# 35 steps of the attention, in place of 18, take their squares from DRAM, transposed at the load; transfer figures of the scheduler changed

## The chip, the cores and the metric

The program runs on one core of a Trainium2 chip. The metric is the device time of one launch in microseconds (us). An execution under the profiler is read beside it. PE is TensorE (matmuls; PEld its weight loads), DVE is VectorE, ACT is ScalarE, POOL is GpSimd, and SP is SyncE, which issues almost every DMA.

## What is computed

```python
scores = scale * np.matmul(z, z.transpose(0, 2, 1))      # batch 4, seq 3072, d_qk 64
attn = np.maximum(scores, 0.0) ** 2                      # symmetric: z against itself
x = u * np.matmul(attn, v)                               # d_model 256
...                                                      # mixture of experts: 8 experts, capacity N // E * 2
...                                                      # keeps the first tokens of each expert, 256 -> 1024 -> 256
...                                                      # second network: 256 -> 2048 -> 256 on every token
```

The matrix `attn` of a batch is symmetric: the block for queries A and keys B is the transpose of the block for queries B and keys A.

## The kernel before, in words

The first part is the attention of the first 3,456 tokens. It runs in seven chunks of queries: chunks 0 to 5 are 512 queries each of the first batch, chunk 6 is 384 queries of the second. A chunk has 24 steps, one for 128 keys. An ordinary step is: two score matmuls of 512 columns (`scores`, L584); on ACT a relu out of PSUM into a tile `own` (L1015) and a square in place (L1021); a cast of the square to the matmul type on ACT or DVE (L113, L940) and, on DVE, the remainder of that cast (`rest`, L116), each into a tile of kind "rounded" (`ownr`, or the tiles `win` and `wout`, lent until chunk 6); and six matmuls that add to the output (`attend`, L124 to L127). Steps are three ahead in scores (`LEAD`).

18 steps have no score of their own. In chunks 3, 4 and 5, for keys that are the queries of chunks 0, 1 and 2, two steps in four are *mirrored*: the square was computed in the earlier chunk with the roles exchanged. There, in 36 source steps, DVE transposes 256 columns of the square in blocks of 32 by 32 (L1035), and four DMAs on SP (`m_store`, L617) write the tile to DRAM (`mir`) in pieces of 128 bytes so that it lies turned. The mirrored step then loads 128 rows of 2 KB with one DMA (`m_load`, L624).

Around this, DVE *narrows* the weights of the second network from 64 bits (`narrowing`, L1293 to L1335): eight loads of 1 MB into `raw` (L1279), each followed by two chains of nine DVE operations and by four stores to DRAM (L1351). Other work of DVE is the routing of each chunk's tokens (L656 to L859). After a chunk its rows are scattered by POOL into expert buffers. After chunk 6 come the first expert, which shares the time with the last routing, and then seven more experts and the second network; none of that is touched by the change.

The order of all this is set by a planner in the kernel (`Conductor`). It holds a list of jobs with a pace (estimated time on the engine), what they wait for, a step by which they are needed (`need`, `tail`), and a step before which they are not begun (`gate`). It plays time forward, gives each engine the job that can start first, and writes instructions in that order. The engines then run the order as it was written, each one in order: one instruction that waits holds up all behind it on its engine. The planner's figures for a DMA are `sync` (SP's time to issue), `moved` (time in the DMA engines) and a latency; they move no data by themselves, only the order.

Of the kernel before, what the change touches and what calls it, by code (L numbers as in the profile page):

```python
# [31 lines left out]
def tile_attn_moe_ffn(  # L32
# [256 lines left out]
    class Job:  # L289

        def __init__(
            self, on, pace, do, after=(), need=None, tail=0.0, gate=0, takes=None, ring=None,
            load=0.0, wait=None, kind="plain",
        ):
            self.on = on if isinstance(on, dict) else {on: pace}
            self.do, self.need, self.tail, self.gate = do, need, tail, gate
            self.takes, self.ring, self.load, self.wait = takes, ring, load, wait
            self.kind = kind
            self.after = [d if isinstance(d, tuple) else (d, 0.0) for d in after if d is not None]
            self.then, self.left, self.end, self.ran, self.buffer = [], 0, None, None, None  # L300
            self.placed = False

    class Conductor:

        SAME, CROSS, LATER = 0.03, 0.07, {"PE": 0.08, "ACT": 0.095, "DVE": 0.09}
        BANKS, WINDOW = 4, 16

# [29 lines left out]
        def spare(self, x):  # L337
            best = None
            for b in self.buffers:
                if b["kind"] != x.kind or b["until"] is not None and self.at >= b["until"]:  # L340
                    continue
                t = 0.0
                for u in b["users"]:
                    if u.end is None:
                        break
                    t = max(t, u.end)
                else:
                    if best is None or t < best[0]:
                        best = (t, b)
            return best  # L350

        def start(self, x, e):
            if x.left or self.at < x.gate:
                return None
            t = self.free[e]
            for d, more in x.after:
                t = max(t, d.end + more + (self.SAME if d.ran == e else self.CROSS))
            if x.wait is not None:
                w = x.wait()
                if w is None:  # L360
                    return None
                t = max(t, w + self.CROSS)
            if x.takes is not None:
                b = self.spare(x)
                if b is None:
                    return None
                t = max(t, b[0] + self.CROSS)
            if x.ring is not None and len(self.rings) >= self.BANKS:
                for u in self.rings[-self.BANKS]:
                    if u.end is None:  # L370
                        return None
                    t = max(t, u.end + self.CROSS)
            return t
# [15 lines left out]
        def choose(self, e):  # L389
# [11 lines left out]
            while live:  # L401
# [8 lines left out]
                else:  # L410
# [3 lines left out]
                    if len(x.on) > 1 and e == "DVE":  # L414
                        other = self.slack("ACT", max(self.free["ACT"], t))
                        if self.slack(e, t + pace, x) < max(0.0, other):
                            live = [c for c in live if c[2] is not x]
                            continue
# [16 lines left out]
        def place(self, e, t, x):  # L435
# [9 lines left out]
            if e == "SP":  # L445
                self.dma = max(self.dma, t + pace) + x.load
                x.end = self.dma + 2.0
            else:
                x.end = t + pace + self.LATER[e]
# [45 lines left out]
    def stage(att, flow):  # L495
# [95 lines left out]

        SOURCES, MIRRORED, MT, MC = (0, 1, 2), (3, 4, 5), QA // P, 2
        lm = flow == "first"
        if lm:
            mir = {
                c: dram.tile([len(MIRRORED), MC * P, QA], F32, name=f"mir{c}") for c in SOURCES
            }
# [12 lines left out]
        def mirrored(c, k):  # L610
            return lm and c in MIRRORED and k // MT in SOURCES and k % MT >= MT - MC

        def m_store(c, k, t):
            m, q = k // MT - MIRRORED[0], k % MT * P
            to = mir[c][m][:, q:q + P].rearrange("(b y) (l p) -> l y b p", y=SQ, p=SQ)
            for l in range(MT):
                nc.sync.dma_start(  # L617
                    out=to[l],
                    in_=t[l * SQ:(l + 1) * SQ].rearrange("y (b p) -> y b p", p=SQ),
                )  # L620

        def m_load(c, k, w):
            r = (k % MT - MT + MC) * P
            nc.sync.dma_start(out=w, in_=mir[k // MT][c - MIRRORED[0]][r:r + P, :])  # L624

# [8 lines left out]
        def route(c, b, q0, nq, accs, us, done, ready, where, freed, last):  # L634
# [215 lines left out]
            chain("g", lambda: nc.vector.reciprocal(out=t["g"], in_=t["g"]), k=20)  # L850
            puts, prior = [], prev
            for j in range(n):
                def scaled(j=j):
                    row, g = t["row"], t["g"]
                    nc.vector.tensor_scalar(
                        out=row[:, j, 0:TOK], in0=row[:, j, 0:TOK], scalar1=g[:, j, :],
                        scalar2=None, op0=ALU.mult,
                    )
                    nc.gpsimd.tensor_copy(  # L859
# [13 lines left out]

                prev = prior
                chain("row", scaled, pace=0.27, k=23)
            return listed

        def mm(n, count=1):
# [14 lines left out]
        def sync(packets):  # L893
            return 0.3 + packets * 0.0009

# [3 lines left out]
        def work(chunks, fresh, more=None, warm=None):  # L899
# [3 lines left out]

            LEAD = 3 if more else 2
            steps = [(c, k) for c in range(len(chunks)) for k in range(NK)]
# [28 lines left out]
            )  # L934

            def cast_by(x, out, src):
                if x.ran == "ACT":
                    rounded(out, src)
                else:
                    nc.vector.tensor_copy(out=out, in_=src)  # L940

# [39 lines left out]
            for i, (c, k) in enumerate(steps):  # L981
# [9 lines left out]
                )  # L991
                source = bool(mirrors) and c in SOURCES and k // MT in MIRRORED
                users = [cast, al]
                if (c, k) in mirrors:
                    w = Job(
                        "SP", sync(P), None, need=a_item, tail=9.0, gate=max(0, a_item - 18),
                        takes=users, load=moved(P, 2048),
                    )

                    def do(buf, s=s, c=c, k=k):  # L1000
                        s["a"] = buf
                        m_load(c, k, s["a"])

                    w.do = do
                else:
# [20 lines left out]
                    if source:  # L1026
                        t = add("DVE", dve_turn(MC * P), None, after=[w], need=a_item, tail=-3.0)
                        users.append(t)
                        put = add("SP", 4 * sync(MC * P), None, after=[t], need=a_item, tail=-3.5,
                                  load=moved(MC * P * 4, 128))  # L1030
                        t.takes = [put]

                        def do(buf, s=s):
                            s["t"] = buf[:, :MC * P]
                            nc.vector.transpose(out=s["t"], in_=s["a"][:, QA - MC * P:QA])  # L1035

                        t.do = do
                        put.do = lambda s=s, c=c, k=k: m_store(c, k, s.pop("t"))
                        stored[c, k] = put
# [17 lines left out]
                before(attended[c, k], cast, (al, -mm(nq, 4)))  # L1057
                if (c, k) in mirrors:
                    before(w, *(stored[k // MT, q] for q in range(c * MT, (c + 1) * MT)))

# [189 lines left out]
        def narrowing(ctx):  # L1250
            W, EVERY = 512, 16
            add, total, chains, loads = ctx["add"], ND * F2 // (2 * 512) + NF2 // 4, {}, []
# [21 lines left out]
            for n in range(total):  # L1274
# [6 lines left out]
                for q in range(2):  # L1281
# [3 lines left out]
                    def op(pace, fn, after=(), takes=None, kind="plain"):  # L1285
                        x = Job("DVE", pace, fn, after=[*ops[-1:], *after], takes=takes, kind=kind)
                        ops.append(x)
                        return x
# [44 lines left out]
                    def o8(buf, t=t):  # L1333
                        t["n0"] = buf
                        nc.vector.tensor_copy(out=buf, in_=t["af"])  # L1335

# [3 lines left out]

                    x1 = op(fast, o1, [load], [])
                    x2 = op(wide, o2)
                    x3 = op(fast, o3, takes=[])
                    x4, x5, x6, x7 = op(wide, o4), op(wide, o5), op(fast, o6), op(wide, o7)
                    x8 = op(fast, o8, takes=[], kind="rounded")
                    x9 = op(wide, o9, takes=[], kind="rounded")
# [22 lines left out]
        def fills(ctx):  # L1369
            add, where = ctx["add"], ctx["where"]  # L1370

# [21 lines left out]
            for i in range(FIRST // NZ):  # L1393
                add("SP", sync(NZ), partial(zero, i), after=[x],
                    gate=where["s", (1, 2 * i)], load=moved(NZ, 1024))

# [413 lines left out]
```

## Time and profile before

| | |
|---|---|
| time, median of 3 runs | 734.85 us (734.74 to 735.48) |
| the profiled execution | 735.21 us, span 733.4 us, mean granted clock 0.997 |
| PE, DVE, ACT busy | 717.3 (98%), 576.2 (79%), 584.5 (80%) us |
| the attention | 0 to about 317 us of the span |
| DMA packets | 151,807, of them 102,150 under 512 B |

The span is from the first to the last instruction of the profiled execution. PE is busy nearly all of it, so a change is felt where it alters what PE has to do or makes it wait. A matmul that the profile shows as 389 ns overlaps the next; how often one starts is the better measure.

### The profile page before, as it was taken

The page shows a single profiled execution, that of the slowest core. Times are in us where ns is not written, and L with a number is a line of the kernel's source. Part 1 is how long each engine was busy: PE and PEld are TensorE (multiplying, and loading weights), DVE is VectorE, ACT ScalarE, POOL GpSimd, SP SyncE. Part 2 cuts the span into 40 slices and gives each one's busy share as a digit, 9 for nine tenths or more (in the row PEclk, how much of TensorE's full clock was granted, in tenths as well). Part 3 has the DMA queues.
Part 4 walks back from the last instruction along what each step waited for, and adds up shares of the span by engine and source line. Part 5 has one row for each costly group of instructions (what it writes and reads, how often), then busy time and mean ns, then how long its engine had stood idle before and what let it go on. Part 6 is the DMA issues. An engine that isn't in the chain of part 4 may idle for free. (4 is left out here: it accounts for less than half of the span.)

```text
span 733.4 us, 11565 instructions
## 1 busy us (share of the span) xinstructions
PE 717.3 (98%) x3800; PEld 646.3 (88%) x3800; DVE 576.2 (79%) x1259; ACT 584.5 (80%) x1188; POOL 67.9 (9%) x108
## 2 busy tenths in 40 slices
PE   8999998999999999999999999999999999999996
PEld 5888886878888889998899999999999999999995
DVE  7988966998998988876967777777777777777782
ACT  7999997878868699957867777777778787788891
POOL 1000202002040120210000101001001001001011
PEclk9999999999999999999999999999999999999998
DMA  7739839487375455507660430710802504300000
GB/s 180 222 61 275 234 61 268 73 212 236 112 206 172 118 168 173 198 26 242 231 180 0 133 91 10 220 16 22 223 1 75 170 0 144 123 1 22 0 23 23
DMA packets 151807, 90.69 MB, mean 124 GB/s; under 512 B 102150, under 2 KB 140588, under 8 KB 151232
## 3 DMA queue, kind: packets, MB, share of 16 engines
q1 hardware_dynamic: 149296, 83.43, 41.2%
q0 software_dynamic: 2448, 6.49, 2.5%
q8 instruction: 31, 0.51, 0.3%
q14 instruction: 32, 0.26, 0.1%
HBM read 52.87 MB, written 35.94 MB: 121 GB/s over the span
## 5 line engine op out<-in xcount | busy, mean ns | idle before, releaser
L1632 PE MATMUL o<-wout,gh 128*128 128x512 f32 x384 | 139.3, 394 | 0.0
L1607 DVE SCALAR_TENSOR_TENSOR t<-x,t 128x384 f32<-128x384 f32 x128 | 71.4, 558 | 83.9 <-ACT t L1604 82.5
L1602 ACT ACTIVATE m<-h 128x384 f32<-128x384 f32 x128 | 62.6, 489 | 68.8 <-PE h L127 68.4
L1636 PE MATMUL o<-wout,gl 128*128 128x256 f32 x384 | 107.2, 280 | 0.2 <-DVE gl L116 0.2
L1015 ACT ACTIVATE own<-s 128x512 f32<-128x512 f32 (+1 forms) x150 | 85.2, 568 | 26.4 <-PE s L584 21.4
L1021 ACT ACTIVATE own<-own 128x512 f32<-128x512 f32 (+1 forms) x150 | 92.2, 615 | 4.2
L124 PE MATMUL h<-xh,win 128*128 128x384 f32 x256 | 86.2, 337 | 0.5 <-DVE g L1610 0.3
L125 PE MATMUL h<-xh,win 128*128 128x384 f32 x256 | 85.6, 334 | 0.0
L1632 PEld LDWEIGHTS o<-wout,gh 128*128 128x128 f32 x384 | 71.9, 188 | 11.1
L1610 DVE SCALAR_TENSOR_TENSOR g<-h,t 128x384 f32<-128x384 f32 x128 | 71.3, 557 | 4.4
L1636 PEld LDWEIGHTS o<-wout,gl 128*128 128x128 f32 x384 | 72.7, 189 | 1.1 <-DVE gl L116 0.9
L1603 ACT ACTIVATE x<-m 128x384 f32<-128x384 f32 x128 | 67.3, 526 | 4.1
L116 DVE TENSOR_TENSOR gl<-g,gh 128x384 fp32r<-128x384 f32 x128 | 70.0, 547 | 0.2 <-ACT gh L113 0.2
L127 PE MATMUL acc<-ownr,vs 128*128 128x512 f32 (+1 forms) x216 | 64.5, 379 | 3.5 <-DVE ownr L116 3.5
L113 ACT ACTIVATE gh<-g 128x384 fp32r<-128x384 f32 x128 | 65.2, 509 | 1.0 <-DVE g L1610 0.9
L127 PE MATMUL h<-xl,win 128*128 128x384 f32 x256 | 65.7, 337 | 0.0
L1604 ACT ACTIVATE t<-m 128x384 f32<-128x384 f32 x128 | 65.1, 508 | 0.0
L584 PE MATMUL s<-zs 128*128 128x512 f32 (+1 forms) x150 | 58.6, 391 | 0.0
L584 PE MATMUL s<-zw,zs 128*128 128x512 f32 (+1 forms) x150 | 57.2, 382 | 0.0
L124 PEld LDWEIGHTS h<-xh,win 128*128 128x128 f32 x256 | 48.0, 188 | 6.3 <-DVE g L1610 1.2
L124 PE MATMUL acc<-ownr,vs 128*128 128x512 f32 (+1 forms) x140 | 52.1, 372 | 0.0
L125 PE MATMUL acc<-ownr,vs 128*128 128x512 f32 (+1 forms) x140 | 51.9, 371 | 0.0
(153 smaller groups left out, 1655.2 us busy)
## 6 DMA issues: line engine op xcount, KB each, us to landing
raw<-in_moe_w_dram SPq DMA_DIRECT2D x16, 1024.0 KB, 6.3
out_dram<-fill SPq DMA_DIRECT2D x32, 384.0 KB, 6.9
vr<-in_v_dram SPq DMA_DIRECT2D x24, 256.0 KB, 4.4
mir<-own SPq DMA_DIRECT2D x144, 32.0 KB, 1.7
own<-mir SPq DMA_DIRECT2D x18, 256.0 KB, 2.8
raw<-in_moe_w_in_dram SPq DMA_DIRECT2D x4, 1024.0 KB, 6.1
raw<-in_moe_w_out_dram SPq DMA_DIRECT2D x4, 1024.0 KB
win<-win_d SPq DMA_DIRECT2D x8, 512.0 KB, 5.6
```

What stands on the lines that cost most here:

```text
L116: nc.vector.tensor_tensor(out=out, in0=src, in1=fp(hi), op=ALU.subtract)
L124: nc.tensor.matmul(out=ps, lhsT=hi, rhs=rh, start=first, stop=False)
L125: nc.tensor.matmul(out=ps, lhsT=lo, rhs=rh, start=False, stop=False)
L127: nc.tensor.matmul(out=ps, lhsT=hi, rhs=rl, start=False, stop=last)
L584: nc.tensor.matmul(out=ps, lhsT=zs[:, k * P:(k + 1) * P], rhs=w, start=(i == 0), stop=(i == 1))
L1015: nc.scalar.activation(out=s["a"][:, :nq], in_=s.pop("ps"), func=ACTF.Relu)
L1021: nc.scalar.activation(out=a, in_=a, func=ACTF.Square)
L1603: nc.scalar.activation(out=self.x, in_=self.m, func=ACTF.Exp, scale=-1.0)
L1607: nc.vector.scalar_tensor_tensor(out=self.t, in0=self.x, scalar=1.0, in1=self.t, op0=ALU.add, op1=ALU.mult)
L1610: nc.vector.scalar_tensor_tensor(out=self.g, in0=self.ps, scalar=0.0, in1=self.t, op0=ALU.max, op1=ALU.add)
L1632: both = lambda: nc.tensor.matmul(out=o, lhsT=hi[:, sl], rhs=w.rearrange("p a d -> p (a d)"), start=(f == 0), stop=(f == NF2 - 1),)
L1636: one = lambda: nc.tensor.matmul(out=o[:, 0:D], lhsT=lo[:, sl], rhs=w[:, 0, :], start=False, stop=False)
```

## The change

It replaces one way of passing a square through DRAM by another and uses it for more steps.

- Which steps: the table `MC` gives, for source chunk and target chunk, how many of each four steps are mirrored (2 or 3). Its 15 entries sum to 35 mirrored steps: 2, 6, 9, 8 and 10 in chunks 1 to 5. (The few words that came with the change say 34.)
- At the source: no DVE transpose. After the square one DMA stores its last 256 or 384 columns as rows of 1,024 or 1,536 bytes. 60 source steps store, 20 of them in chunk 0.
- At the target: four DMAs, each of 512 pieces of 128 bytes, load the tile with its blocks in turned places, and DVE transposes 512 columns in place, block by block (L1020 of the new file). Loads may begin 13 items ahead of the step (18 before).
- Figures: `sync` is 0.32 + 0.00034 us a packet (0.3 + 0.0009 before), landing is counted 2.5 us after the transfer (2.0), and SP jobs that no step needs wait until the planner's DMA queue is all but empty.
- Narrowing: its first operation is placed 4.0 us after the planned landing of its `raw` load; a load comes every 14 steps (16); its buffers are taken only where more than two are free (`modest`); its cast may go to ACT. The scaling of routed rows may go to ACT as well. The clause with `EASE` = 9.0 asks whether `slack` exceeds 9.0, which is the most that `slack` returns.
- The nine writes of zeros to the output (`out_dram<-fill`) that stood in chunk 1 and just behind it are allowed from chunk 6 on.

```diff
+                    spares += 1
                     if best is None or t < best[0]:
                         best = (t, b)
-            return best
+            return best if spares > x.modest else None
...
+            if e == "SP" and x.need is None:
+                t = max(t, self.dma - 0.5)
...
-                        if self.slack(e, t + pace, x) < max(0.0, other):
+                        if other > self.EASE or self.slack(e, t + pace, x) < max(0.0, other):
...
-                x.end = self.dma + 2.0
+                x.end = self.dma + 2.5
...
-        SOURCES, MIRRORED, MT, MC = (0, 1, 2), (3, 4, 5), QA // P, 2
+        MT = QA // P
+        MC = {(0, 1): 2, (0, 2): 3, (1, 2): 3, (0, 3): 3, (1, 3): 3, (2, 3): 3, (0, 4): 2, (1, 4): 2, (2, 4): 2, (3, 4): 2, (0, 5): 2, (1, 5): 2, (2, 5): 2, (3, 5): 2, (4, 5): 2}
...
         def mirrored(c, k):
-            return lm and c in MIRRORED and k // MT in SOURCES and k % MT >= MT - MC
-
-        def m_store(c, k, t):
-            m, q = k // MT - MIRRORED[0], k % MT * P
-            to = mir[c][m][:, q:q + P].rearrange("(b y) (l p) -> l y b p", y=SQ, p=SQ)
-            for l in range(MT):
+            return lm and k % MT >= MT - MC.get((k // MT, c), 0)
+
+        def m_store(c, k, a):
+            to = mir[c, k // MT]
+            r = k % MT * P
+            nc.sync.dma_start(out=to[r:r + P, :], in_=a[:, QA - MC[c, k // MT] * P:QA])
+
+        def m_load(c, k, w):
+            n = MC[k // MT, c]
+            x = (k % MT - MT + n) * P
+            for s in range(0, P, SQ):
                 nc.sync.dma_start(
-                    out=to[l],
-                    in_=t[l * SQ:(l + 1) * SQ].rearrange("y (b p) -> y b p", p=SQ),
-                )
-
-        def m_load(c, k, w):
-            r = (k % MT - MT + MC) * P
-            nc.sync.dma_start(out=w, in_=mir[k // MT][c - MIRRORED[0]][r:r + P, :])
+                    out=w[s:s + SQ].rearrange("p (t y) -> p t y", y=SQ),
+                    in_=mir[k // MT, c][:, x + s:x + s + SQ].rearrange("(t p) y -> p t y", p=SQ),
+                )
...
-            return 0.3 + packets * 0.0009
+            return 0.32 + packets * 0.00034
...
-            LEAD = 3 if more else 2
+            LEAD, AHEAD = (3 if more else 2), 13
...
-                source = bool(mirrors) and c in SOURCES and k // MT in MIRRORED
+                source = bool(mirrors) and MC.get((c, k // MT))
                 users = [cast, al]
                 if (c, k) in mirrors:
-                    w = Job(
-                        "SP", sync(P), None, need=a_item, tail=9.0, gate=max(0, a_item - 18),
-                        takes=users, load=moved(P, 2048),
+                    w = Job("DVE", dve_turn(nq), None, need=a_item, tail=1.5)
+                    users.append(w)
+                    load = add(
+                        "SP", 4 * sync(nq), None, need=a_item, tail=8.0, gate=max(0, a_item - AHEAD),
+                        takes=users, load=moved(4 * nq, 128),
+                        after=[stored[k // MT, q] for q in range(c * MT, (c + 1) * MT)],
                     )
                     def do(buf, s=s, c=c, k=k):
                         s["a"] = buf
-                        m_load(c, k, s["a"])
+                        m_load(c, k, buf)
+
+                    load.do = do
+                    before(w, load)
+
+                    def do(s=s):
+                        nc.vector.transpose(out=s["a"], in_=s["a"])
...
-                        t = add("DVE", dve_turn(MC * P), None, after=[w], need=a_item, tail=-3.0)
-                        users.append(t)
-                        put = add("SP", 4 * sync(MC * P), None, after=[t], need=a_item, tail=-3.5,
-                                  load=moved(MC * P * 4, 128))
-                        t.takes = [put]
-
-                        def do(buf, s=s):
-                            s["t"] = buf[:, :MC * P]
-                            nc.vector.transpose(out=s["t"], in_=s["a"][:, QA - MC * P:QA])
-
-                        t.do = do
-                        put.do = lambda s=s, c=c, k=k: m_store(c, k, s.pop("t"))
+                        put = add("SP", sync(P), None, after=[w], need=a_item, tail=-1.0,
+                                  load=moved(P, source * 512))
+                        users.append(put)
+                        put.do = lambda s=s, c=c, k=k: m_store(c, k, s["a"])
                         stored[c, k] = put
...
-            W, EVERY = 512, 16
+            W, EVERY = 512, 14
...
-                    x1 = op(fast, o1, [load], [])
+                    x1 = op(fast, o1, [(load, 4.0)], [])
...
+                    x8.on["ACT"] = act(W)
...
-                    gate=where["s", (1, 2 * i)], load=moved(NZ, 1024))
+                    gate=where["s", (last, 2 * i)], load=moved(NZ, 1024))
```

What the change does to the order is shown at three places. PE at the start of chunk 3, from the transposition of chunk 2's tokens (`xps`) on; `s` is a score, `acc` the output, `vs_144` holds the values of keys 2 and 3 of the chunk. Before:

```order
L670 MATMUL xps<-iw,ur 128x136 x8
L584 MATMUL s<-zs 128x512
L584 MATMUL s<-zw,zs 128x512
L124 MATMUL acc_1746<-ownr_180,vs_144 128x512
L125 MATMUL acc_1746<-ownr_180,vs_144 128x512
L124 MATMUL acc_1747<-ownr_180,vs_144 128x512
L125 MATMUL acc_1747<-ownr_180,vs_144 128x512
L127 MATMUL acc_1746<-ownr_176,vs_144 128x512
L127 MATMUL acc_1747<-ownr_176,vs_144 128x512
```

And now:

```order
L676 MATMUL xps<-iw,ur 128x136 x8
L124 MATMUL acc_1656<-ownr_187,vs_144 128x512
L125 MATMUL acc_1656<-ownr_187,vs_144 128x512
L124 MATMUL acc_1657<-ownr_187,vs_144 128x512
L125 MATMUL acc_1657<-ownr_187,vs_144 128x512
L127 MATMUL acc_1656<-wout_173,vs_144 128x512
L127 MATMUL acc_1657<-wout_173,vs_144 128x512
```

The pair of score matmuls ahead of the step belonged to step 5 of the chunk; that step is now mirrored, as three of each four are here, and the pair is gone. Over the program PE has 34 rows fewer, all of them scores.

SP around the start of chunk 3 (`mir` is the squares in DRAM, `win_d` the narrowed weights). Before:

```order
L617 DMA mir_157<-own_167 32x8x32 x4
L624 DMA own_173<-mir_157 128x512
L624 DMA own_171<-mir_157 128x512
L1351 DMA win_d<-wout_161 128x2x256
L1351 DMA win_d<-ownr_179 128x2x256
```

And now:

```order
L627 DMA own_182<-mir_158 32x16x32 x4
L621 DMA mir_167<-own_183 128x256
L621 DMA mir_167<-own_178 128x256
L621 DMA mir_167<-own_184 128x256
L627 DMA own_177<-mir_159 32x16x32 x4
L627 DMA own_183<-mir_159 32x16x32 x4
L627 DMA own_178<-mir_159 32x16x32 x4
L627 DMA own_184<-mir_160 32x16x32 x4
L627 DMA own_180<-mir_160 32x16x32 x4
L627 DMA own_182<-mir_160 32x16x32 x4
L574 DMA ur<-in_u_dram 32x32x32 x4
```

Two loads of one DMA each became a run of six loads of four; with the three ahead of it (the first row is the last of these) and five stores in between, all nine loads of chunk 3 stand there without other work.

DVE where the third 1 MB piece of weights (`raw_116`) is first used. Before, in chunk 2's routing (`idx`, `g`: the places and gates of chunk 1's tokens):

```order
L840 TENSOR_TENSOR idx<-ps_1364,over 128x4
L1293 TENSOR_SCALAR own_163<-raw_116 128x512
L846 TENSOR_REDUCE g<-dl 128x4
L1293 TENSOR_SCALAR own_171<-raw_116 128x512
L849 TENSOR_SCALAR g<-g 128x4
L116 TENSOR_TENSOR ownr_178<-own_164,wout_161 128x512
```

And now, near the end of chunk 1:

```order
L116 TENSOR_TENSOR win_170<-own_180,win_170 128x512
L116 TENSOR_TENSOR ownr_191<-own_184,ownr_189 128x512
L1302 TENSOR_SCALAR own_185<-raw_116 128x512
L1302 TENSOR_SCALAR own_178<-raw_116 128x512
L116 TENSOR_TENSOR ownr_190<-own_183,wout_171 128x512
```

The same two operations stand more than half a chunk earlier, away from the routing. On DVE, 35 transposes of 512 columns (L1020) stand where 36 of 256 (L1035) stood; 11 of 24 row scalings have left DVE for ACT.

## Rows read from the trace of the kernel before

**Rows 1.** Seven stretches of about a chunk: length, busy time of each engine, clock, DMA share

```profile
54.00:99.00 45.00, 45.00 (x209) 37.41 (x209) 36.41 (x87) 42.85 (x76) 5.11 (x9) 1.00 0.83 219
99.00:151.00 52.00, 48.53 (x220) 38.93 (x218) 41.85 (x102) 43.87 (x76) 5.50 (x9) 1.00 0.63 143
151.00:193.00 42.00, 41.90 (x192) 34.38 (x193) 37.24 (x90) 35.93 (x66) 4.85 (x9) 1.00 0.68 203
193.00:235.00 42.00, 42.00 (x196) 34.96 (x195) 39.43 (x96) 32.95 (x60) 10.15 (x9) 1.00 0.59 174
235.00:280.00 45.00, 45.00 (x223) 37.30 (x223) 40.51 (x100) 36.15 (x66) 6.95 (x9) 1.00 0.54 155
280.00:318.00 38.00, 37.87 (x225) 37.13 (x224) 30.28 (x87) 32.76 (x71) 5.03 (x8) 1.00 0.51 163
```

**Rows 2.** PE in order of time: start, duration, what, and the wait before it

```profile
112.02 0.39 PE L124 MATMUL acc<-wout,vs 128*128 128x512 f32 x1
112.24 0.39 PE L125 MATMUL acc<-wout,vs 128*128 128x512 f32 x1
...
116.32 0.39 PE L125 MATMUL acc<-wout,vs 128*128 128x512 f32 x1
119.65 0.73 PE L127 MATMUL acc<-ownr,vs 128*128 128x512 f32 x2 [2.94 <-DVE ownr L116]
```

**Rows 3.** DVE in order of time, around the same place

```profile
118.07 0.43 DVE L1293 TENSOR_SCALAR own<-raw 128x512 int32<-128x512 int32 x1 [6.51 <-DMA raw<-in_moe_w_in_dram]
...
118.91 0.68 DVE L116 TENSOR_TENSOR ownr<-own,wout 128x512 fp32r<-128x512 f32 x1
```

**Rows 4.** SP in order of time: start, time to issue, what, how many

```profile
65.39 7.58 SPq L570 DMA_DIRECT2D ur<-in_u_dram  x4
...
111.51 0.69 SPq L1279 DMA_DIRECT2D raw<-in_moe_w_in_dram  x1
...
143.06 0.45 SPq L624 DMA_DIRECT2D own<-mir  x1
143.61 1.87 SPq L617 DMA_DIRECT2D mir<-own  x4
...
295.67 1.44 SPq L143 DMA_DIRECT2D raw<-in_moe_w_dram  x2
```

**Rows 5.** The same view, where nothing else was in SP's queue

```profile
198.83 2.87 SPq L570 DMA_DIRECT2D ur<-in_u_dram  x4
```

**Rows 6.** Groups of 0 to 300 us: busy, mean ns, idle before and what ended it

```profile
L1021 ACT ACTIVATE own<-own 128x512 f32<-128x512 f32 x126 | 79.6, 632 | 3.6
L1015 ACT ACTIVATE own<-s 128x512 f32<-128x512 f32 x126 | 73.7, 585 | 25.6 <-PE s L584 21.1 <-DMA mir<-own 1.1 <-DVE own L1035 1.0
L1035 DVE STREAM_TRANSPOSE own<-own 128x256 f32<-128x256 f32 x36 | 15.7, 437 | 2.3 <-ACT own L1021 2.3
L579 DVE STREAM_TRANSPOSE ur<-ur 128x512 f32<-128x512 f32 x12 | 8.1, 693 | 0.0
```

**Rows 7.** DVE in order of time, narrowing and remainders without gaps

```profile
147.47 1.29 DVE L116 TENSOR_TENSOR ownr<-own,ownr 128x512 fp32r<-128x512 f32 x2
148.67 0.44 DVE L1035 STREAM_TRANSPOSE own<-own 128x256 f32<-128x256 f32 x1
149.03 0.38 DVE L940 CAST wout<-own 128x512 fp32r<-128x512 f32 x1
```

**Rows 8.** DMA of 199.4 to 203.6 us, the four loads of Rows 5 alone

```profile
DMA packets 4101, 0.53 MB, mean 127 GB/s; under 512 B 4093, under 2 KB 4093, under 8 KB 4101
...
q1 hardware_dynamic: 4101, 0.53, 85.6%
```

**Rows 9.** DMA issues of the whole run: count, KB each, median us to landing

```profile
mir<-own SPq DMA_DIRECT2D x144, 32.0 KB, 1.7
own<-mir SPq DMA_DIRECT2D x18, 256.0 KB, 2.8
```

**Rows 10.** ACT's first use of the first expert's weights

```profile
307.06 0.63 ACT L113 ACTIVATE w1hl<-raw 128x512 fp32r<-128x512 f32 x1
```

More of the change, by code (lines that the diff above doesn't have):

```diff
@@ L293, in __init__ @@
             load=0.0, wait=None, kind="plain",
+            modest=0,
         ):
@@ L297, in __init__ @@
             self.takes, self.ring, self.load, self.wait = takes, ring, load, wait
-            self.kind = kind
+            self.kind, self.modest = kind, modest
             self.after = [d if isinstance(d, tuple) else (d, 0.0) for d in after if d is not None]
@@ L305, in tile_attn_moe_ffn @@
         SAME, CROSS, LATER = 0.03, 0.07, {"PE": 0.08, "ACT": 0.095, "DVE": 0.09}
-        BANKS, WINDOW = 4, 16
+        BANKS, WINDOW, EASE = 4, 16, 9.0
         def __init__(self, items, jobs, buffers, clocks):
@@ L337, in spare @@
         def spare(self, x):
-            best = None
+            best, spares = None, 0
             for b in self.buffers:
@@ L595, in stage @@
             mir = {
-                c: dram.tile([len(MIRRORED), MC * P, QA], F32, name=f"mir{c}") for c in SOURCES
+                sm: dram.tile([QA, n * P], F32, name=f"mir{sm[0]}{sm[1]}") for sm, n in MC.items()
             }
@@ L850, in route @@
             chain("g", lambda: nc.vector.reciprocal(out=t["g"], in_=t["g"]), k=20)
-            puts, prior = [], prev
+            puts, prior, scales = [], prev, {}
             for j in range(n):
@@ L854, in scaled @@
                     row, g = t["row"], t["g"]
-                    nc.vector.tensor_scalar(
-                        out=row[:, j, 0:TOK], in0=row[:, j, 0:TOK], scalar1=g[:, j, :],
-                        scalar2=None, op0=ALU.mult,
-                    )
+                    r = row[:, j, 0:TOK]
+                    if scales[j].ran == "ACT":
+                        nc.scalar.activation(out=r, in_=r, func=ACTF.Copy, scale=g[:, j, :])
+                    else:
+                        nc.vector.tensor_scalar(
+                            out=r, in0=r, scalar1=g[:, j, :], scalar2=None, op0=ALU.mult
+                        )
                     nc.gpsimd.tensor_copy(
@@ L872, in scaled, with cast_by @@
                     puts.append(put)
-                prev = prior
-                chain("row", scaled, pace=0.27, k=23)
-            return listed
+                both = {"DVE": 0.27, "ACT": act(TOK)} if c < last else "DVE"
+                scales[j] = put("row", both, 0.27, prior, 23)(scaled)
+            return listed
+        def cast_by(x, out, src):
+            if x.ran == "ACT":
+                rounded(out, src)
+            else:
+                nc.vector.tensor_copy(out=out, in_=src)
         def mm(n, count=1):
@@ L934, in work @@
             )
[L936 to L940, printed above, removed]
             def score_item(c, k):
@@ L1057, in work @@
                 before(attended[c, k], cast, (al, -mm(nq, 4)))
-                if (c, k) in mirrors:
-                    before(w, *(stored[k // MT, q] for q in range(c * MT, (c + 1) * MT)))
             def keys(b, c, loads, begun):
@@ L1285, in op @@
                     def op(pace, fn, after=(), takes=None, kind="plain"):
-                        x = Job("DVE", pace, fn, after=[*ops[-1:], *after], takes=takes, kind=kind)
+                        x = Job("DVE", pace, fn, after=[*ops[-1:], *after], takes=takes, kind=kind,
+                                modest=2)
                         ops.append(x)
@@ L1334, in o8 @@
                         t["n0"] = buf
-                        nc.vector.tensor_copy(out=buf, in_=t["af"])
+                        cast_by(t["x8"], buf, t["af"])
                     def o9(buf, t=t):
@@ L1344, in narrowing @@
                     x4, x5, x6, x7 = op(wide, o4), op(wide, o5), op(fast, o6), op(wide, o7)
-                    x8 = op(fast, o8, takes=[], kind="rounded")
+                    x8 = t["x8"] = op(fast, o8, takes=[], kind="rounded")
+                    x8.on["ACT"] = act(W)
                     x9 = op(wide, o9, takes=[], kind="rounded")
@@ L1369, in fills @@
         def fills(ctx):
-            add, where = ctx["add"], ctx["where"]
+            add, where, last = ctx["add"], ctx["where"], len(ctx["chunks"]) - 1
             def gate_weights():
```

## The prediction

> **What bounds the kernel now.** I read the stretches first, one per chunk [rows 1]. In five of the six PE is busy for the whole length, at a granted clock of 1.00 (the 2.4 GHz level). Only in chunk 2, from 99 to 151 us, is it busy for 48.53 of 52.00 us. DVE has 2 to 10 us free in each stretch and ACT 2 to 9, so both are close behind. Busy alone does not say that PE is at its pace, so I went to its order in time. There a 512-column matmul starts 0.22 to 0.23 us after the last (112.02, 112.24) [rows 2], against a shown duration of 0.39. I take 0.227, which is 24 attending steps of six of them in 32.7 us, and with 24 pairs of scores 43.6: about what a stretch without stalls lasts. So the attention runs at the pace of the matmuls, and a score that is not computed is time won, as long as nothing else comes late.
>
> The 3.5 us lost in chunk 2 have one main cause. A matmul that should follow 116.32 by 0.227 us starts at 119.65, 3.1 us late, behind a remainder from DVE [rows 2]. DVE stood for 6.51 us before the first narrowing operation, which waited for its 1 MB of weights [rows 3]. That load was issued at 111.51 [rows 4] and used from 118.07. The planner had DVE stand behind a transfer that it believed to be done earlier, and everything in order behind it was late, the remainder that PE wanted (118.91) with it.
>
> **The change, part by part.** The base is the profiled execution, 735.2 us, 0.05% over the median of 734.85; span 733.4 and 1.8 around it.
>
> *Scores.* 35 mirrored steps for 18: 17 steps x 2 matmuls = 34 fewer, which is also what the order of PE shows. 34 x 0.227 = 7.7 us. Bounds: 0 if PE waits instead, 7.7 at most. I take -7.7.
>
> *The narrowing wait.* The planner now counts 0.4 us to issue, 3.6 for the transfer (128 x 8 pieces of 1,024 bytes by its formula), 2.5 to land and 4.0 more: 10.5 us, where the trace needed 118.07 - 111.51 = 6.6. It would take another 4 us of delay on SP to bring the wait back. I take -3.1 (bounds 0 and -3.5, all that chunk 2 lost).
>
> *ACT.* 17 relus of 0.585 and 17 squares of 0.632 us go [rows 6], 20.7 us; 11 row scalings and some casts come. ACT was free at times already, so this is worth nothing by itself; it is cover for casts.
>
> *DVE.* Without gaps a 512-column remainder takes (148.67 - 147.47) / 2 = 0.60 us, a 256-column transpose 149.03 - 148.67 = 0.36 [rows 7]. A 512-column transpose shows 693 ns against 437 for the half [rows 6]; less the overlap of some 0.07 it takes 0.62. So 35 x 0.62 - 36 x 0.36 = +8.7 us; 11 row scalings leave (0.27 each by their pace in the planner, -3.0), two casts come (+0.7). Net +6.4 us, of which chunk 0 gets -4.3 or more and the six stretches some +10.7: 237 us on 226. The trouble is where it falls. The old transposes lay in chunks 0 to 2. Of the new ones 8 each lie between the gates (the first operations of the routing) of chunks 2 and 3, 3 and 4, 4 and 5. From the gate of chunk 3 to that of chunk 4 the new order has on DVE 45 operations of 0.60 (remainders and slow narrowing), 8 transposes of 0.62, 19 casts and fast narrowing operations at 0.335, two transposes of `ur`, one row scaling, and 24 small ones at 0.1 (these by their paces): 42.2 us. PE has 176 matmuls x 0.227 and the transposition of the tokens, 1.8 by its pace: 41.7 us. So here DVE has no slack at all, and what it waits PE will wait. Before, the same count gave 37.5 us on DVE. Bounds of the cost: nothing, as ten lent and seven own rounded tiles hold work eight steps ahead; or all the waits that DVE gets.
>
> *SP.* A load is four DMAs of 512 pieces. One of 128 pieces took 0.45 us to issue, one of 256 took 1.87 / 4 = 0.47 [rows 4], one of 1,024 took 2.87 / 4 = 0.72 [rows 5]. Between the last two, 512 lie at 0.55: 2.2 us a load, where the planner counts 1.98. Stores cost 0.45 instead of four times 0.47. The tight place is the run of nine loads and five stores ahead of chunk 3: 9 x 2.2 + 5 x 0.45 = 22.0 us. PE gives it this long: six steps of chunk 2 at 8 x 0.227 = 1.8 us from where the gate (13 items) opens, 10.9; then twelve steps of chunk 3, nine of six matmuls and three of eight, 17.7; less some 6.5 for the last load, 4 to land (a plain load takes 2.8 [rows 9], this one issues for longer) and 2.5 for transpose, cast and remainder: 22.1 us. It fits with nothing to spare. Behind it on SP stand `ur` and the next `zw`, with half a chunk of room.
>
> *DMA engines.* The gather of `ur` has the same 128-byte pieces. 4,101 packets in 4.2 us at 85.6% of 16 engines are 14.0 ns each [rows 8], so 2,048 packets are 1.8 us a load, 63 us in all. Gone are 144 writes of 256 packets and 18 loads of 256 KB [rows 9], 32 us at the same 14.0 ns and 21 at the 219 GB/s of chunk 1's stretch, the busiest [rows 1]. The 60 stores carry 35 x 256 KB, 42 us at that rate. Net +52 us; the six stretches hold 167 us of DMA in 264, so the share goes from 0.63 to about 0.8. Hidden if loads are issued early, and the gate of 13 items does that. The Trainium skill (VectorE: DVE Perf Modes, section The three transpose paths) warns that a plain DMA copy that transposes by strides is 19 times slower than the crossbar's. By that rule, as an estimate from that page, a load would hold the engines for 19 x 1.2 us (256 KB at 219 GB/s) and 35 loads for 800 us, a kernel of over 1,300. The trace disagrees: pieces of 128 bytes out of rows of 1 KB went at 14.0 ns. I give this case under 0.01.
>
> *Zeros.* Nine writes of 384 KB leave chunk 1 (share 0.83) for chunk 6 (0.51) [rows 1]. At the 219 GB/s of chunk 1 they are 1.8 us each, 16 in 38 us: it fits. The first expert's weights are issued at 295.67 and used at 307.06 [rows 4, 10]; a write ahead of them costs 1.8 of these 11.4 us. I take 0 (bound +2).
>
> *Sum.* For new waits I put 1.5 us: 0.5 by which DVE exceeds PE in chunk 4 (42.2 against 41.7), and 1.0 for a load or two that come late in chunk 3, where SP has nothing to spare. 735.2 - 7.7 - 3.1 + 1.5 = **725.9**. What follows chunk 6 is untouched and moves forward whole.
>
> **Rivals.** *Late squares.* DVE stands at a transpose whose load has not landed, as it did at the weights. For: no slack in chunk 4 on DVE, none in chunk 3 on SP. Against: the gate lets a load begin 13 items, some 12 us, before its step, and a plain one landed after 2.8 [rows 9]. If one load in five is 0.8 us late where DVE has no slack, 7 x 0.8 = 5.6 us come in place of 1.5: 730.
>
> *Slow issue, the other sign.* With transfers ahead of it in the queue, SP took 7.58 us for the four loads of `ur` [rows 4], 1.9 each; half of that for 512 pieces is 0.95, 3.8 a load. The run ahead of chunk 3 then takes 9 x 3.8 + 2.3 = 36.5 in place of 22: 14 us. By the same count the six loads of chunk 2 have about 17 us, with 2.3 of stores, and overrun by 8; the eight of chunk 4 (31 us, 6 of other work) by 5, the ten of chunk 5 (37, 7.5) by 8.5. It decides from about 3.0 us a load, where the overruns are 7.6, 3.3, 0 and 0.5: over the 9.3 that I expect to win. Half-way, at 3.3, they are 10, 5, 1.4 and 3.5: 725.9 + 20 - 1.5 = 744. For it: the share of 0.7 to 0.9. Against: the nine zero writes that filled the queue at 65 us are no longer there, and SP jobs that no step needs wait for an empty queue.
>
> *Nothing won.* The freed matmuls are spent waiting for DVE, and the narrowing wait comes back elsewhere: 735. DVE's 237 us in the six stretches, against 253 that would be left of their 264, speak against it.
>
> *More.* All stalls of chunk 2 go and none comes: 735.2 - 7.7 - 3.5 = 724.0; a further 2 us, if the smaller losses of the six stretches go too, gives 722.
>
> **How the numbers follow.** The forecast of 725.9, from 723.5 to 728.5, has 0.60. Late squares (728.5 to 733.7) 0.18; more than forecast (under 723.5) 0.06; nothing won 0.06; slow issue 0.10. A difference under 0.2%, 1.5 us, is about what a measurement of this kernel cannot tell from none. Faster 0.60 + 0.18 + 0.06 = 0.84, same 0.06, slower 0.10. The range from 722 to 734.5 leaves out half of "nothing won", most of slow issue, and some of "more": under 0.2.
>
> **What would show it.** Right: PE busy throughout chunk 2, no wait of DVE on `raw` over 1 us, 133 score pairs in place of 150, the last attending matmuls near 307 us instead of 317, and the rest as long as before. The issue of the 140 loads should have a median near 0.55 us. Wrong: waits of DVE's transpose on `own<-mir` that add up to more than 5 us, or of PE on remainders in chunks 3 to 5 (late squares); an issue of 0.75 us or more and SP without a gap from chunk 2 to 5 (slow issue); a first expert that starts later against the end of chunk 6 (zeros).

## The result, and the profile after

The changed kernel takes 723.32 us (median of 4 runs, 723.20 to 724.02) against 734.90 for the kernel before, measured beside it: a ratio of 0.9843 with a 95% interval of 0.9826 to 0.9860. That is 11.6 us faster; forecast were 9.3. The span went from 733.4 to 721.6 us. All of it lies in the attention: the last gate (L656 before, L662 now) starts at 305.4 us in place of 317.2, and what follows is as long as before.

The stretches after, with the lengths that the chunks have now, in the form of [rows 1]:

```profile
54.00:99.00 45.00, 45.00 (x210) 37.41 (x209) 41.01 (x96) 40.09 (x72) 5.84 (x9) 1.00 0.83 220
99.00:147.00 48.00, 48.00 (x230) 40.14 (x229) 43.60 (x98) 38.93 (x73) 5.41 (x9) 1.00 0.77 190
147.00:188.00 41.00, 41.00 (x189) 33.99 (x188) 38.31 (x92) 31.41 (x57) 6.04 (x9) 1.00 0.84 201
188.00:229.00 41.00, 41.00 (x188) 33.92 (x187) 40.56 (x97) 31.64 (x60) 14.61 (x9) 1.00 0.73 165
229.00:271.00 42.00, 41.48 (x210) 34.78 (x209) 39.46 (x98) 31.99 (x62) 6.13 (x9) 1.00 0.93 228
271.00:307.00 36.00, 35.47 (x215) 35.02 (x214) 27.52 (x81) 29.99 (x66) 4.87 (x8) 1.00 0.68 215
```

PE is busy for the whole of chunk 2 (99 to 147 us), where 3.5 us were lost [rows 1]. DVE (third pair of numbers) is busy for 40.56 of 41 us in chunk 4, and the DMA share is 0.80 over these 253 us, 0.63 before. So the change did fill DVE and the queue as counted. PE still does not wait for either there. What it waits for is in its order of time, in the form of [rows 2]:

```profile
257.86 0.50 PE L539 MATMUL zps<-identr,t 128*128 128x128 f32 x4 [0.52 <-ACT own L1039]
...
301.54 0.85 PE L217 MATMUL dps<-ident,rows 128*128 128x128 f32 x6 [0.53 <-DMA rows<-disp]
```

These two are the only waits that the profile shows for PE from 12 us to the end of the attention. One is for the keys of the second batch behind ACT, one for the rows of the first expert.

The new instructions, by line (duration shortest, median, longest; first and last start):

```profile
L588 PE MATMUL s<-zs x133: 333/389/818, 5.8 to 299.5; 128*128 128x512 f32 x109, 128*128 128x384 f32 x24
...
L627 SPq DMA_DIRECT2D own<-mir x140: 303/487/1751, 43.8 to 246.4; - x140
...
L621 SPq DMA_DIRECT2D mir<-own x60: 314/346/1211, 16.3 to 223.4; - x60
...
L1020 DVE STREAM_TRANSPOSE own<-own x35: 667/705/717, 49.3 to 249.9; 128x512 f32<-128x512 f32 x35
```

133 pairs of scores and 35 turns, as counted. A load's DMA took 487 ns to issue where I had 550. The run ahead of chunk 3, in SP's order of time as in [rows 4], where six loads stand together:

```profile
138.28 1.41 SPq L621 DMA_DIRECT2D mir<-own  x3
139.78 12.70 SPq L627 DMA_DIRECT2D own<-mir  x24
152.58 3.02 SPq L574 DMA_DIRECT2D ur<-in_u_dram  x4
```

24 DMAs in 12.70 us are 0.53 each, 2.1 us a load. SP works there without a gap. PE does not wait for it; ACT waits once, for one of these loads:

```profile
148.31 0.64 ACT L113 ACTIVATE win<-own 128x512 fp32r<-128x512 f32 x1 [0.92 <-DMA own<-mir]
```

### The profile page after: what moved, and what is told of

Read it like the earlier page. It is cut to its first block, busy times and chain, and to the rows that moved or that the text cites. A ratio compares the mean times of both kernels' runs of the same rounds, so it can differ in the third digit from the quotient of the medians.

```text
span 721.6 us, 11560 instructions
## 1 busy us (share of the span) xinstructions
PE 708.1 (98%) x3766; PEld 640.7 (89%) x3766; DVE 579.3 (80%) x1249; ACT 564.1 (78%) x1163; POOL 72.9 (10%) x108
## 5 line engine op out<-in xcount | busy, mean ns | idle before, releaser
L1033 ACT ACTIVATE own<-s 128x512 f32<-128x512 f32 (+1 forms) x133 | 75.5, 568 | 24.3 <-PE s L588 22.3
L1039 ACT ACTIVATE own<-own 128x512 f32<-128x512 f32 (+1 forms) x133 | 81.2, 611 | 3.2
L1642 PEld LDWEIGHTS o<-wout,gh 128*128 128x128 f32 x384 | 71.9, 188 | 11.2
L588 PE MATMUL s<-zs 128*128 128x512 f32 (+1 forms) x133 | 51.9, 390 | 0.0
L1661 POOL DMA_INDIRECT out_dram<-oy,toks x21 | 20.7, 984 | 297.7 <-DVE oy L1660 267.1
```

The source lines that it names most:

```text
L1033: nc.scalar.activation(out=s["a"][:, :nq], in_=s.pop("ps"), func=ACTF.Relu)
L1039: nc.scalar.activation(out=a, in_=a, func=ACTF.Square)
L1642: both = lambda: nc.tensor.matmul(out=o, lhsT=hi[:, sl], rhs=w.rearrange("p a d -> p (a d)"), start=(f == 0), stop=(f == NF2 - 1),)
```

## The experiments

Two theories at the start. *Pace*: PE runs at 0.227 us a matmul, so the time changes by the matmuls left out and by PE's waits alone. *Order*: the gain is a better plan (figures, margins, relief of DVE and SP), and the number of mirrored steps matters little. Ratios are to the kernel before on the same chip; the changed kernel is at 0.9843, and 0.001 is 0.73 us.

**The same matmuls put back.** Every other instruction stands in the order of the changed kernel.

```diff
-            for i, w in enumerate((zs[:, q0:q0 + nq], zw[:, 0:nq])):
+            twice = lm and (k in (8, 12, 20, 22) and q0 in (512, 1024, 1536, 2048) or (k, q0) == (8, 2560))
+            for i, w in list(enumerate((zs[:, q0:q0 + nq], zw[:, 0:nq]))) * (2 if twice else 1):
```

> The changed kernel with 17 of its score pairs computed twice into the same bank (four steps each in chunks 1 to 4, one in chunk 5; the result is the same). The planner does not know of them, so every other instruction stands in the same order. Pace theory: 34 matmuls x 0.227 = +7.7 us over the changed kernel, less what falls into its few waits (1.4 us): 729.6 to 731.0 us. Rival (PE has room, the gain came from the other edits): under 726.

Measured: 730.77 us, ratio 0.9948 (0.9934 to 0.9962): 0.0105 or 7.7 us over the changed kernel. 34 matmuls at 0.227 us are 7.7. Pace holds for this term to within its interval of about 1 us; PE has no room in the attention into which they could fall.

**Only the margin.** The kernel before, with `x1 = op(fast, o1, [(load, 4.0)], [])`.

> The kernel before, with one figure changed: the first narrowing operation is planned 4.0 us after its weights land. Pace theory (PE runs at 0.227 us a matmul, so time comes only from matmuls left out and from waits of PE): the 6.5 us wait of DVE in chunk 2 goes, and with it 3.1 to 3.5 us: about 731.6 us, PE busy throughout chunk 2. Rival (the new order as a whole made the gain): the wait moves to another place and the time stays at 735.

Measured: 738.59 us, ratio 1.0037 (1.0021 to 1.0053), slower. The wait did not go. DVE in order of time:

```profile
120.36 0.76 DVE L1293 TENSOR_SCALAR own<-raw 128x512 int32<-128x512 int32 x2 [4.67 <-DMA raw<-in_moe_w_in_dram]
...
126.46 1.30 DVE L579 STREAM_TRANSPOSE ur<-ur 128x512 f32<-128x512 f32 x2 [4.14 <-DMA ur<-in_u_dram]
```

And SP ahead of it:

```profile
113.55 0.49 SPq L1279 DMA_DIRECT2D raw<-in_moe_w_in_dram  x1
114.09 0.65 SPq L486 DMA_DIRECT2D out_dram<-fill  x1
114.84 8.28 SPq L570 DMA_DIRECT2D ur<-in_u_dram  x4
```

DVE stands first for the weights and then for `ur`, whose four loads took SP 8.28 us, against 2.87 where nothing else was in the queue [rows 5]. In front of these loads stand 1 MB of weights and a write of zeros. PE lost 2.07 and 4.05 us against its pace of 0.227 us a matmul behind the two waits. DVE came to the weights at 115.69 (120.36 less 4.67), 4.1 us later than before (118.07 less 6.51 [rows 3]), but SP issued them 2.0 us later as well (113.55 against 111.51 [rows 4]). A margin in the plan moves the instruction that waits; it does not bring the transfer forward.

**Only the zeros.** The kernel before, with the writes of zeros gated at `where["s", (last, 2 * i)]`.

> The kernel before, with one edit of the change: the nine writes of zeros allowed from chunk 6 on, not from chunk 1. Theory: the wait of DVE on the weights in chunk 2 came from a full DMA queue, and the zeros helped to fill it; without them the wait and its 3.1 us go: about 731.8 us. Rival: the queue there is filled by the old stores and the narrowing, the wait stays within 2 us of 6.5: 734 to 736.

Measured: 731.06 us, ratio 0.9952 (0.9938 to 0.9966): 3.5 us faster. No wait on the weights is left, and PE is busy throughout chunk 2:

```profile
99.00:151.00 52.00, 52.00 (x248) 43.53 (x247) 48.42 (x114) 47.31 (x85) 5.52 (x9) 1.00 0.62 150
```

One edit, of which I had written that it is worth nothing, takes away what I had put down to the margin. SP's order shows how. In the kernel before, eight of the nine writes stand on SP between 63.62 and 82.12 us and take it 8.35 us to issue; behind them come 48 stores of squares, and then the weights at 111.51 [rows 4]:

```profile
73.01 4.75 SPq L486 DMA_DIRECT2D out_dram<-fill  x5
82.23 27.14 SPq L617 DMA_DIRECT2D mir<-own  x48
```

Without the zeros the same stores begin 6.5 us earlier, and the weights are issued 10 us earlier, while DVE comes to them at the same time as before (111.49 against 111.56):

```profile
75.70 23.70 SPq L617 DMA_DIRECT2D mir<-own  x48
101.55 0.68 SPq L1279 DMA_DIRECT2D raw<-in_moe_w_in_dram  x1
```

```profile
111.49 0.43 DVE L1293 TENSOR_SCALAR own<-raw 128x512 int32<-128x512 int32 x1
```

My theory named a full DMA queue. What the weights waited behind was SP's time to issue. In the kernel before, the DMA engines are busy for only 0.39 of the stretch ahead of them (DMA share, the last number but one):

```profile
90.00:108.00 18.00, 18.00 (x88) 15.21 (x88) 10.87 (x27) 17.26 (x32) 0.55 (x4) 1.00 0.39 62
```

The 3.5 us here, measured on the kernel before, and the 7.7 us of scores, measured on the changed kernel, sum to 11.2 of the 11.6 us.

**The changed kernel without one of these.** Without the margin (`[load]`), with the zeros back in chunk 1, and without the rule for SP jobs that no step needs:

```diff
-            if e == "SP" and x.need is None:
-                t = max(t, self.dma - 0.5)
```

> The changed kernel without the 4.0 us that the narrowing keeps from its weights. Pace theory, if the margin is what removed the wait: a wait of DVE on the weights is back at one or more of the eight pieces and costs up to 3.1 us: about 726 us. Rival (the pieces come earlier now, with the zeros out of chunk 1 and 2.5 us counted to land): no wait over 1 us, 723.3.

> The changed kernel with the nine writes of zeros allowed from chunk 1 again. Theory (zeros, late, are what removed the wait on the weights): the queue in chunks 1 and 2 is full again, with 52 us more of DMA than before in the attention, and DVE waits for weights or squares: 726 us or more, with such a wait over 2 us in chunk 1 or 2. Rival (the figures and the margin would have kept the wait away without it): within 1.5 us of 723.3.

> The changed kernel without the rule that SP jobs no step needs wait until the planner's DMA queue is all but empty. Theory (place of the zeros decides, this rule does not): within 1.5 us of 723.3. Rival: weights, zeros and narrowing stores crowd in front of the loads of squares; DVE or PE waits of over 2 us, 726 or more.

Measured: 724.30 us, ratio 0.9852 (0.9834 to 0.9869); 724.42, 0.9849 (0.9835 to 0.9862); 725.34, 0.9865 (0.9850 to 0.9881). The first two are the same as the changed kernel within their intervals. The third is 1.6 us above it with intervals that overlap, between what its two sides expected. In none does DVE wait over 0.6 us for weights. My theory that the zeros' place is what keeps the wait away holds for the kernel before and falls for the changed one: with the zeros back its chunks 1 and 2 have a DMA share of 0.91 and 0.88 and no lost time:

```profile
54.00:99.00 45.00, 45.00 (x209) 37.45 (x208) 39.85 (x93) 40.91 (x75) 5.84 (x9) 1.00 0.91 256
99.00:147.00 48.00, 48.00 (x230) 40.22 (x229) 42.91 (x96) 40.09 (x75) 5.61 (x9) 1.00 0.88 220
```

So none of these three edits alone brings the wait back in the changed plan, and what keeps it away there is open: the edits may cover for each other, or it is another part of the new order. One sign: with the zeros back, the nine writes stand apart on SP, one or two at a time, and take it 4.5 us in all, where they took 9.0 in the kernel before. The zeros back without the rule for SP jobs, both at once, were not run.

**The new way with the old 18 steps.**

```diff
-        MC = {(0, 1): 2, (0, 2): 3, (1, 2): 3, (0, 3): 3, (1, 3): 3, (2, 3): 3, (0, 4): 2, (1, 4): 2, (2, 4): 2, (3, 4): 2, (0, 5): 2, (1, 5): 2, (2, 5): 2, (3, 5): 2, (4, 5): 2}
+        MC = {(s, m): 2 for s in range(3) for m in range(3, 6)}
```

> The changed kernel, with the table cut to the 18 steps of before (two of four, keys of chunks 0 to 2, chunks 3 to 5). All else as changed: rows stored, squares turned at the load, figures, margins. Pace theory: 34 matmuls are back, +7.7 us: 731.0 us. Rival (the gain is DVE and SP relieved of the old stores, and a better order): 724 to 726, as the steps beyond 18 only fill time that PE would wait.

Measured: 734.46 us, ratio 0.9988 (0.9976 to 0.9999): 10.7 us over the changed kernel and 2.6 over the kernel before with its zeros late. 7.7 of the 10.7 are the matmuls. Of the other 3.0 most are waits of PE. The first:

```profile
195.00 0.50 PE L588 MATMUL s<-zs 128*128 128x512 f32 x1 [1.04 <-ACT row L690]
```

Here ACT, copying a chunk's tokens, had to wait until POOL's scatter of the last chunk had read its buffer, and the next scores waited for the bank. Two waits at the keys of the second batch (0.25 us at 262.94, 1.29 at 265.27) and one for the first expert's rows (0.66) come on top: 3.2 us, where the changed kernel has 1.05. So 2.2 of the 3.0 us are seen. All other edits together gain next to nothing at 18 steps; the steps beyond 18 gain. Whether the 3 us belong to the transport or to this one plan is open; the three variants before this one have 0.6 to 1.9 us of such waits.

**More steps.** 39 and 45 mirrored steps, by the table alone (three of four for more pairs of chunks):

> The changed kernel with 39 mirrored steps: three of four also for chunk 0 into 1, 4 and 5 and chunk 2 into 4. Pace theory: 8 matmuls fewer, -1.8 us: 721.5, if no wait comes. From the 45 steps I expect instead that the plan's own waits grow at the end of chunks 4 to 6: 723 to 727.

> The changed kernel, with three of four steps mirrored for every pair of chunks: 45 steps, not 35. Pace theory: 20 matmuls fewer, -4.5 us: 718.8 us. Rival (DVE has no slack left in chunks 3 to 5, SP none ahead of a run of loads): ten more turns of 0.62 us make PE wait for DVE, and the time is 722 or more, with waits of PE or its weight loads on remainders in chunks 4 and 5.

Measured: 724.35 us, ratio 0.9843 (0.9829 to 0.9856), the same as with 35; and 733.01, 0.9964 (0.9951 to 0.9977), 8.9 us slower than with 35. Pace would give -1.8 and -4.5 us. With 39 steps one wait, behind ACT's copying of a chunk's tokens, is as long as what 8 matmuls would win:

```profile
274.48 0.44 PE L588 MATMUL s<-zs 128*128 128x384 f32 x1 [1.77 <-ACT row L690]
```

With 45 steps PE waits in seven places from 143 us on, for casts, remainders and the keys of the second batch, 0.2 to 1.5 us each, and then at the end for the first expert's rows:

```profile
311.04 1.54 PE L217 MATMUL dps<-ident,rows 128*128 128x128 f32 x6 [3.08 <-DMA rows<-disp]
```

The rival's bound (722 or more) held, its place in part: some of the waits are on DVE's work. The longest is for rows whose load SP issues only at 307.36, after narrowing stores and zeros; that these make it late is read from the order and was not tried. Neither table beats the changed kernel.

**The turns left out.** `nc.vector.transpose(out=s["a"], in_=s["a"])` becomes `pass`; nothing else moves.

> The changed kernel with the 35 transposes of squares left out (the output differs; nothing else moves, the planner still counts them). It measures what 35 x 0.62 = 21.7 us of DVE cost. Pace theory: they are hidden, and what is left of waits in chunks 1 to 5 is under 1 us: 722.3 to 723.5. If DVE, level with PE in chunk 4, holds PE up: 720 or less.

Measured: 723.31 us, ratio 0.9834 (0.9821 to 0.9848), not to be told from the changed kernel. In chunk 4 DVE is then busy for 37.42 us, with the turns for 40.56:

```profile
188.00:229.00 41.00, 41.00 (x188) 33.95 (x188) 37.42 (x90) 31.49 (x59) 6.46 (x9) 1.00 0.79 173
```

So the 35 turns, some 21.7 us of DVE in all, are hidden whole, also in chunk 4, where DVE is 99% busy with them.

**The loads' cover.** Every turned load issued twice (a second `m_load(c, k, buf)`), and a lead of 6 items (`AHEAD` 13 to 6):

> The changed kernel with every turned load issued twice (eight DMAs of 512 pieces, not four). SP then needs about 4.1 us a load, the case of my slow-issue rival. By its count the runs ahead of chunks 2 to 5 overrun by 9, 17, 7 and 11 us: some 44 us more, about 765 us, with PE waiting for remainders in each chunk. If the loads have far more cover than I counted: under 735.

> The changed kernel, in which a turned load may begin 6 items ahead of its step, not 13. If the lead is what hides the loads: a load needs some 6.5 us to the remainder, 6 items are 5 us, so that each run of loads costs PE a few us: 735 us or more. Rival (the rounded tiles ahead of PE hide it, or SP starts loads late anyway): under 727.

Measured: 814.53 us, ratio 1.1076 (1.1055 to 1.1096), and 732.32, 0.9963 (0.9950 to 0.9975). With loads of 8 DMAs DVE stands at the turns (waits: total, times, longest), and SP works through 48 DMAs in a row:

```profile
DVE own L1021 <- DMA own<-mir: 79.4, 32, 4.7
```

```profile
171.07 27.33 SPq L627 DMA_DIRECT2D own<-mir  x48
```

27.33 / 48 = 0.57 us each, 4.6 a load. The slow-issue rival names a real cliff: +91 us, twice the 44 that its formula gave. The formula counted waits alone. PE's idle time rises by 61 us (13.5 to 74.5), and the same 3,766 matmuls keep PE busy for 740.2 us in place of 708.1, at a mean granted clock of 0.953 against 0.999: PE runs slow for a while after some waits (last section). Why the waits are 61 us and not 44 was not tried; the formula took each chunk's overrun by itself, though SP starts the next chunk's stores and loads later as well. At 2.1 us a load the changed kernel stands on the safe side of the cliff. The lead of 13 items is part of that. With 6, the time lies between what the two sides expected: one wait of 2.85 us in chunk 3 and what comes of it, and smaller ones in chunks 4 and 5, take 8.8 us back.

## Why the prediction was right, step by step

The largest term was right in size and cause. The second came out in size while its cause was wrong, which is luck in part. The time of 723.3 lies just under the main range (723.5 to 728.5), in the case "more than forecast" that had 0.06.

- *Scores, -7.7.* Right, and shown: 7.7 us come back with the 34 matmuls alone.
- *The narrowing wait, -3.1.* The size was right (3.5 shown, the upper bound that I gave from chunk 2), the cause of its going was wrong. The step said that the planner's 4.0 us take it away. They do not: alone they make the kernel slower, and without them the changed kernel is the same. Moving the nine writes of zeros is enough on the kernel before, as SP then issues the weights 10 us earlier. What took the wait away in the changed kernel itself stays open. The 3.5 are the wait of 3.1 and a smaller one that the kernel before has at 151.00 (0.53 us). The step looked at the plan's figure against the 6.6 us of one load, and not at when SP would come to issue it.
- *Zeros, 0.* Wrong for the same reason: their price was looked for in chunk 6, where they go, and not in chunks 1 and 2, which they leave. On the kernel before their move is worth 3.5 us; on the changed one putting them back costs 0.4, which is not clear of noise.
- *ACT, 0.* Nothing in the runs speaks against it; it was not tried by itself.
- *DVE, level with PE in chunk 4.* The count was right there (42.2 us forecast between gates of 42.6 us; busy 40.56 of 41 in the stretch), though over the six stretches DVE has 230.5 us and not 237. The 0.5 us taken for it was not seen: leaving out all turns gains nothing that can be measured. Longer waits of DVE do reach PE: with the loads issued twice DVE waits 79.4 us at its turns, and PE idles 61 us more. That the lead of eight steps hides the short ones is the likely reason and was not tried.
- *SP.* 2.1 us a load (2.2 forecast), a run without a gap ahead of chunk 3, and no wait of PE behind it. Right.
- *DMA.* 0.80 of the engines (0.8 forecast), hidden. Right, with 202 us of transfers in the six stretches against 219 (167 + 52) forecast. The Trainium skill (VectorE: DVE Perf Modes, section The three transpose paths) gives its factor of 19 for a large innermost stride in the destination. The pieces here are 128 bytes long on both sides, so the 14.0 ns do not speak against that factor, and no run here tests it.
- *New waits, +1.5.* The two seen are 0.7 us each, of PE against its pace, but in chunks 5 and 6, not in 3 and 4. With the small losses that went the term is near 0. Of the 2.6 us between 725.9 and 723.3 this makes 1.5, the 3.5 in place of 3.1 makes 0.4, and the base, measured at 734.9 where I had 735.2, makes 0.3; the last 0.4 is within the noise. The measured time is nearest to the case that I called "more" (724.0 with all stalls of chunk 2 gone and none new).
- *Rivals.* Late squares did not come, with 487 ns a DMA. Slow issue did not come but exists; its sum at 3.0 us a load has a slip (9 x 3.0 + 2.3 less 22.1 is 7.2, not 7.6) that changes nothing. "Nothing won" is excluded by the scores put back.

## What to carry to other kernels

Where one engine runs at its pace, count what is left out on that engine and trust it; then prove it by putting exactly that work back and nothing else. A wait on a transfer belongs to everything that its issuing engine does first: before giving its removal to a margin in a plan, ask when the transfer was issued and what stood ahead of it, above all what nothing needs soon. An engine that is 99% busy need not be a bottleneck: taking 3.1 us of DVE's work out of chunk 4 gained nothing here. And a queue that copes at 2 us a load can cost 90 us at 4.6.

## What the runs showed of the hardware that was not expected

PE's granted clock halves around some waits of 2 to 4 us and not around others. In the run with a lead of 6, PE waits until 163.03 (2.70 us idle), and the stretches show the clock around it:

```profile
163.03 0.79 PE L124 MATMUL acc<-win,vs 128*128 128x512 f32 x1 [2.70 <-DVE win L891]
```

```profile
162.40:169.20 6.80, 6.17 (x15) 4.81 (x16) 5.41 (x12) 1.86 (x3) 0.00 (x0) 0.50 0.78 242
169.20:176.00 6.80, 6.80 (x31) 5.61 (x30) 5.31 (x17) 5.99 (x11) 0.00 (x0) 1.00 0.07 24
```

For 6.8 us the level is 1.2 GHz, and PE does 15 matmuls where the next 6.8 us hold 31: 16 x 0.227 = 3.6 us lost. The first 0.6 us of the stretch are the end of the wait itself, so some 3.0 us come on top of a wait of 2.85. The run with the margin alone shows it after a wait of 4.05 us (3.4 us at the lower level), the one with 45 steps around its wait of 3.25 us (6.8 us):

```profile
128.30:131.70 3.40, 3.30 (x8) 2.63 (x9) 3.40 (x9) 1.16 (x2) 0.00 (x0) 0.50 0.25 78
```

```profile
310.50:317.30 6.80, 6.26 (x25) 5.79 (x25) 2.63 (x6) 1.76 (x4) 0.00 (x0) 0.50 0.46 166
```

The kernel before, after its wait of 3.1 us [rows 2], keeps the full level:

```profile
119.60:126.60 7.00, 6.95 (x31) 5.72 (x31) 7.00 (x16) 5.53 (x10) 4.37 (x4) 1.00 1.07 249
```

The run with 39 steps has some 3.3 us at the lower level after a shorter wait, of 1.77 us until 274.48, and only when PE had worked again for 1.4 us:

```profile
275.90:279.20 3.30, 3.30 (x12) 3.30 (x11) 2.70 (x11) 2.02 (x5) 0.60 (x4) 0.50 0.81 182
```

So the length of the wait alone does not tell whether the clock falls: idle times of 1.77, 2.70, 3.08 and 3.88 us came with the lower level, one of 2.94 did not. Why is open. Such a wait cost PE itself or, with the clock, up to some twice itself, so single waits of this length can be worth removing beyond their own size.
